# A three-part float32 product on one core: cross terms that read the upper halves of the float32r words in place

## The chip, the cores and the metric

The kernel runs on one core of one Trainium2 chip. The metric is the device time of one execution in microseconds. Three runs of the kernel before took 2292.56, 2293.05 and 2294.24 us: median 2293.05. One execution was recorded by the hardware profiler; its own time was 2294.02 us, and the span of its trace is 2292.2 us. The terms PE (TensorE's products), PEld (its weight loads), DVE (VectorE), ACT (ScalarE), POOL (GpSimd) and SP (SyncE, which issues the DMAs) are those of the profile.

## What is computed

For 8 sequences of 4096 tokens with 192 channels, a convolution with 7 taps per token and head (the taps are a softmax of `weight_gen`), and then a feed-forward layer with the activation h cos h:

```python
w = np.exp(weight_gen - max) ; w = w / (sum(w) + 1e-9)        # per token, head: 7 taps
attn = einsum('bshk,bskhg->bshg', w, the 7 last tokens of x)   # 8 heads of 24 channels
x = attn.reshape(32768, 192)
h = x @ w_in            # 192 x 2048
g = h * np.cos(h)
out = g @ w_out         # 2048 x 192
```

The weights `w_in` and `w_out` come as 64-bit floats; the kernel reads their words as integers and makes float32 values of them.

## The kernel before, in words

**Precision.** PE multiplies float32r words (float32 storage, rounded) or bf16 half-words. To come near float32, each factor is split in two: a high part in float32r and a low part, the rest, in bf16. A product x w is then x_hi w_hi in float32r plus two cross terms in bf16, x_lo times w_hi and x_hi times w_lo. A bf16 product needs both factors in bf16, so the high parts exist twice: `x_hi` (float32r) and `x_b` (a bf16 copy of it), `wa_hi` and `wa_b`, `wb_hi` and `wb_b`. The weight copies are made once, by `two_parts` (L118 to L144): ACT writes the high part (L141) and, if asked, the bf16 copy (L143), and POOL the low part (L144). The copy of x is made in `split` (L294 to L302) for each piece: ACT rounds to x_hi (L296), POOL writes x_b (L298 to L300), POOL or DVE writes x_lo (L301).

**Tiling.** The 32768 tokens are worked in NB = 64 batches of 512 tokens. The 2048 columns of `w_in` are 16 chunks of 128, taken as 8 pairs, so the main loop (L575) has 64 x 8 = 512 steps i, and some more to drain. PE works with two halves of 64 rows beside each other; the 192 channels are three pieces of 64 rows. `wa_*` holds channels so that a pair of products covers two of the three pieces, `wb_*` the remaining one of each chunk.

**One step on PE** (`products`, L597). `ffn_in_first` (L330) makes the first chunk's share: 3 pairs of products of 512 columns, in the order wa_b with x_lo, wa_lo with x_b, wa_hi with x_hi (L339). `ffn_in_second` (L345) makes 6 pairs (L356): wa_b x_lo, wa_lo x_b, wb_b x_lo, wb_lo x_b, wa_hi x_hi, wb_hi x_hi. `ffn_out` (L407, products at L430) multiplies what was finished LAG = 8 steps earlier: per step 8 pairs of 384 columns with the float32r part `ghi`, and 8 pairs of 192 columns with the bf16 part `glo`. In three of four steps the order is: the float32r part and half of the bf16 part of `ffn_out`, then `ffn_in_first`, the other half, `ffn_in_second`. In every fourth it is `ffn_in_first`, all of `ffn_out`, `ffn_in_second`. In a row of transposes (L318) PE also turns two rows of a later batch in spare columns of the accumulator.

**Beside PE.** For each step ACT writes the rounded number of turns (L366), the sine (L374) and the float32r part of g (L384); DVE the fraction of a turn (L370), the product g (L377) and the low part (L388). ACT also empties and clears accumulators (L446, L447, L452). POOL computes the attention of a later batch (L255 and L270), the split of the transposed rows (L298, L301) and the sum of the two halves of the output (L461).

**Order.** The program's order on every engine is the order in which the code emits it; manual dependencies at the end (L665 on) keep it. Each engine works its queue in that order. In the first steps the conversions of the later weight pieces are spread over steps 1 to 8 by the list `late` (L501), between the other work of ACT, DVE and POOL. Batches 1 and 2 are transposed whole and split at step 5 of the batch before (L591, L639), the later ones row by row.

Of the kernel before, what the change touches and what calls it, by code (L numbers as in the profile page):

```python
# [11 lines left out]
F32 = mybir.dt.float32  # L12
# [3 lines left out]
BF16 = mybir.dt.bfloat16  # L16
AF = mybir.ActivationFunctionType
ALU = mybir.AluOpType
AX = mybir.AxisListType

P = 128
# [22 lines left out]
def tile_softmax_conv_then_cos_ffn(  # L44
# [8 lines left out]
    nc = tc.nc  # L53
# [5 lines left out]
    F = w_in.shape[1]  # L59
# [4 lines left out]
    CT = R * P  # L64
# [13 lines left out]
    const = ctx.enter_context(tc.tile_pool(name="const", bufs=1))  # L78
    gpool = ctx.enter_context(tc.tile_pool(name="gpool", bufs=12))
    work = ctx.enter_context(tc.tile_pool(name="work", bufs=2))  # L80
# [12 lines left out]

    wa_hi = const.tile([P, F], F32R, name="wa_hi")
    wa_lo = const.tile([P, F], BF16, name="wa_lo")
    wa_b = const.tile([P, F], BF16, name="wa_b")

    wb_hi = const.tile([P, F // 2], F32R, name="wb_hi")  # L100
    wb_lo = const.tile([P, F // 2], BF16, name="wb_lo")
    wb_b = const.tile([P, F // 2], BF16, name="wb_b")
    wo = const.tile([P, NFC, 2 * D], F32R, name="wo")
    wo_b = const.tile([P, NFC, D], BF16, name="wo_b")

    def words(n):

        raw = gpool.tile([P, 2 * CW], I32, name="raw", tag="ghi")
        return raw[:, 0:2 * n]
# [8 lines left out]
    def two_parts(raw, hi, lo, half=None):  # L118
        shape = hi.shape[1:]
        n = math.prod(shape)  # L120

        def shaped(t, steps):
            t = t.rearrange("p (n s) -> p n s", s=steps)
            return t if len(shape) == 1 else t.rearrange("p (a b) s -> p a b s", b=shape[1])

        low, top = (shaped(raw, 2)[..., k] for k in range(2))
        size, bits = (shaped(t[:, 0:n], 1)[..., 0] for t in room.pop(0))
        nc.scalar.activation(out=size.bitcast(F32), in_=top.bitcast(F32), func=AF.Abs, scale=F64_SCALE)
        yield
        nc.vector.tensor_scalar(  # L130
            out=size, in0=size, scalar1=3, scalar2=None, op0=ALU.logical_shift_left)
        yield

        nc.vector.scalar_tensor_tensor(
            out=size, in0=top, scalar=-0x80000000, in1=size, op0=ALU.bitwise_and, op1=ALU.bitwise_or)
        yield

        nc.vector.scalar_tensor_tensor(
            out=bits, in0=low, scalar=29, in1=size, op0=ALU.logical_shift_right, op1=ALU.bitwise_or)
        yield  # L140
        nc.scalar.copy(out=hi, in_=bits.bitcast(F32))  # L141
        if half is not None:
            nc.scalar.copy(out=half, in_=bits.bitcast(F32))  # L143
        nc.gpsimd.tensor_tensor(out=lo, in0=bits.bitcast(F32), in1=hi.bitcast(F32), op=ALU.subtract)  # L144

    def w_in_a(c0, c1):
        raw = words(c1 - c0)
        for n in range(2):
            nc.sync.dma_start(out=raw[n * D2:(n + 1) * D2],
                              in_=w_in[n * P:n * P + D2, c0:c1].bitcast(I32))  # L150
        return two_parts(raw, wa_hi[:, c0:c1], wa_lo[:, c0:c1], wa_b[:, c0:c1])

    w_in_odd_even = w_in.rearrange("k (a n c) -> n k a c", n=2, c=P)

    def w_in_b(j):
        raw = words(CW)
        pairs = slice(j * CW // P, (j + 1) * CW // P)
        for n in range(2):
            nc.sync.dma_start(out=raw[n * D2:(n + 1) * D2].rearrange("k (a c) -> k a c", c=2 * P),
                              in_=w_in_odd_even[1 - n, D2:P, pairs, :].bitcast(I32))  # L160
        cols = slice(j * CW, (j + 1) * CW)
        return two_parts(raw, wb_hi[:, cols], wb_lo[:, cols], wb_b[:, cols])

    w_out_v = w_out.rearrange("(c p) d -> p c d", p=P)

# [120 lines left out]
    def parts_of(b):  # L286
        if b not in xT:
            hi = work.tile([P, 2, CT], F32R, name="x_hi")
            lo = work.tile([P, 2, CT], BF16, name="x_lo")
            near = work.tile([P, 2, CT], BF16, name="x_b")  # L290
            xT[b] = (hi, lo, near)
        return xT[b]

    def split(b, t, cs, eng):  # L294
        hi, lo, near = parts_of(b)
        nc.scalar.copy(out=hi[:, :, cs], in_=t)  # L296
        yield
        nc.gpsimd.tensor_scalar(  # L298
            out=near[:, :, cs], in0=hi[:, :, cs].bitcast(F32), scalar1=1.0, scalar2=1.0,
            op0=ALU.mult, op1=ALU.mult)  # L300
        eng.tensor_tensor(  # L301
            out=lo[:, :, cs], in0=t, in1=hi[:, :, cs].bitcast(F32), op=ALU.subtract)  # L302

# [136 lines left out]
    def evacuate(j):  # L440
# [13 lines left out]
        if k in (1, 3) and row:  # L454
            bt, r = row
            splits.append(split(bt, t, slice(r * P, (r + 1) * P), nc.gpsimd))
# [38 lines left out]
    def all_of(*steps):  # L495
# [4 lines left out]

    late = [  # L501
        (-1, 1, w_in_a, (768, 1280)), (-1, 2, w_in_b, (1,)), (-1, 2, w_out_2, (0,)),
        (0, 3, w_in_a, (1280, 1792)), (0, 3, w_out_2, (1,)), (1, 4, w_out_2, (2,)),
        (1, 4, w_out_2, (3,)), (2, 5, w_in_a, (1792, 2048)),
        (2, 5, w_out_2, (4,)), (4, 6, w_out_2, (5,)), (4, 7, w_out_2, (6,)),
        (5, 8, w_out_2, (7,)),
# [16 lines left out]
    next(sm0)  # L523
    load_rows(0)
    w_b0 = w_in_b(0)
    w_a0 = w_in_a(0, 256)
    sm1 = softmax(R, 3 * R, nc.gpsimd)
# [7 lines left out]
    def go_on(steps, n):  # L535
        for _ in range(n):
# [4 lines left out]
                      t=own_taps.rearrange("p (r h) k -> p r h k", h=H))  # L541
# [17 lines left out]
    go_on(w_a1, 1)  # L559
    all_of(mix_v)  # L560
    first = split(0, transpose_all(0), slice(0, CT), nc.vector)
    go_on(sm2, 2)
    go_on(w_a1, 3)
# [11 lines left out]
    for i in range(N + LAG + 1):  # L575
# [60 lines left out]
        if whole is not None:  # L636
            t = work.tile([P, 2, CT], F32, name="part", bufs=2)
            nc.scalar.copy(out=t, in_=whole)
            later.append(split(b + 1, t, slice(0, CT), nc.vector))  # L639
# [64 lines left out]
```

## Time and profile before

| | |
|---|---|
| median of the runs | 2293.05 us (2292.56 to 2294.24) |
| profiled execution, own time | 2294.02 us |
| its span | 2292.2 us |
| mean granted TensorE clock | 0.984 |
| busy: PE, PEld, DVE, ACT, POOL | 2187.0, 1679.2, 1903.1, 1860.6, 1860.8 us |
| DMA: HBM read, written | 76.50 MB, 25.17 MB |

How to read the lines. In a group, "out<-in" names the tiles, then partitions x elements and type, the count, busy time and mean nanoseconds of one, and the idle time just before with what ended it. "64*128" are the rows and columns of PE that a product uses. In a timeline a line has the start, the length, the engine, the line of the code, and in brackets how long the engine had been idle and what it had waited for. The starts and ends of products are modelled: they are pipelined, so the starts of two that follow each other say more than the length of one. A wait names an engine and line, then the one it waited for: total, times, longest.

### The profile page before, as it was taken

How to read it: one execution, taken by the hardware profiler on the slowest of the kernel's cores; microseconds unless marked ns; L12 is line 12 of the kernel's file. 1: busy time of each engine (PE TensorE's matmuls, PEld its weight loads, DVE VectorE, ACT ScalarE, POOL GpSimd, SP SyncE). 2: the span in 40 equal slices, each digit the busy share in tenths (PEclk: the TensorE clock that was granted, in tenths of full speed). 3: DMA queues.
4: the chain of work that ended last, by engine and by line, in shares of the span. 5: the costliest groups of instructions: out<-in, count | busy, mean ns of one | idle time of the engine just before them, and what ended most of it. 6: DMA issues, size and time to landing. Idle time of an engine off the chain costs nothing.

```text
span 2292.2 us, 61619 instructions
## 1 busy us (share of the span) xinstructions
PE 2187.0 (95%) x26472; PEld 1679.2 (73%) x26472; DVE 1903.1 (83%) x1644; ACT 1860.6 (81%) x2254; POOL 1860.8 (81%) x1583
## 2 busy tenths in 40 slices
PE   2699999999999999999999999999999999999998
PEld 1477777777777777777777777777777777777777
DVE  7788888878888888888888888888888888888886
ACT  4688888888888888887888888888888888888885
POOL 8788878888888878879888888878879888788730
PEclk8799999999999999999999999999999999999999
DMA  6221221211211221221211211111121211212100
GB/s 154 56 54 29 50 54 29 58 46 29 58 47 37 50 49 35 50 55 29 58 40 36 54 40 47 47 43 44 47 49 38 54 33 46 54 33 48 29 15 18
DMA packets 34847, 105.61 MB, mean 46 GB/s; under 512 B 3742, under 2 KB 23702, under 8 KB 34574
## 3 DMA queue, kind: packets, MB, share of 16 engines
q1 hardware_dynamic: 34574, 101.68, 18.5%
q8 instruction: 207, 3.39, 0.6%
q14 instruction: 66, 0.54, 0.1%
HBM read 76.50 MB, written 25.17 MB: 44 GB/s over the span
## 4 chain that ended last, share of the span: by engine, by line
PE 83%; ACT 7%; DVE 7%; issue 2%; POOL 1%; DMA 0%; SPq 0%; ACTq 0%; DVEq 0%
PE acc L430 42%; PE h L356 25%; PE h L339 13%; DVE turn L370 3%; ACT turn L366 3%; DVE glo L388 2%; ACT part L452 1%; PE acc L318 1%; ACT turn L374 1%; ACT ghi L384 1%; DVE den L214 1%; ACT acc L447 0%; ACT xrow L446 0%; POOL xa L270 0%; PE h L430 0%
## 5 line engine op out<-in xcount | busy, mean ns | idle before, releaser
L370 DVE TENSOR_TENSOR turn<-h,turn 128x1024 f32<-128x1024 f32 x512 | 625.9, 1222 | 302.0 <-ACT turn L366 301.9
L430 PE MATMUL acc<-wo,ghi 64*128 64x384 f32 x8096 | 821.6, 341 | 3.6 <-ACT acc L447 2.5
L430 PEld LDWEIGHTS acc<-wo,ghi 64*128 64x128 f32 x8096 | 726.2, 186 | 89.0 <-ACT acc L447 56.4
L270 POOL TENSOR_TENSOR xa<-xa,pr 128x768 f32<-128x768 f32 (+1 forms) x384 | 698.2, 1818 | 0.7
L374 ACT ACTIVATE turn<-turn 128x1024 f32<-128x1024 f32 x512 | 542.0, 1059 | 186.6 <-DVE turn L370 184.8
L366 ACT ACTIVATE turn<-h 128x1024 int32<-128x1024 f32 x512 | 525.9, 1027 | 194.3 <-PE h L356 176.9
L377 DVE SCALAR_TENSOR_TENSOR h<-h,turn 128x1024 f32<-128x1024 f32 x512 | 631.0, 1232 | 54.4 <-ACT turn L374 54.4
L388 DVE TENSOR_TENSOR glo<-h,ghi 128x1024 bf16<-128x1024 f32 x512 | 622.0, 1215 | 10.1 <-ACT ghi L384 10.1
L255 POOL TENSOR_TENSOR pr<-xt,taps 128x768 f32<-128x768 f32 (+1 forms) x384 | 588.3, 1532 | 8.3
L384 ACT CAST ghi<-h 128x1024 fp32r<-128x1024 f32 x512 | 516.7, 1009 | 9.7 <-DVE h L377 9.7
L430 PE MATMUL acc<-wo_b,glo 64*128 64x192 bf16 x8096 | 489.0, 245 | 0.1
L430 PEld LDWEIGHTS <-glo 64*128 64x128 bf16 (+1 forms) x8128 | 315.9, 95 | 118.6 <-issue 100.5
L298 POOL TENSOR_SCALAR x_b<-x_hi 128x256 bf16<-128x256 f32 (+1 forms) x247 | 102.9, 417 | 261.8 <-ACT x_hi L296 261.8
L339 PE MATMUL h<-x_hi,wa_hi 64*128 64x512 f32 x1024 | 302.9, 587 | 0.0
L356 PE MATMUL h<-x_hi,wa_hi 64*128 64x512 f32 x1024 | 302.7, 586 | 0.0
L339 PE MATMUL h<-x_lo,wa_b 64*128 64x512 bf16 x1024 | 198.3, 382 | 71.0 <-DVE glo L388 66.1
L356 PE MATMUL h<-x_hi,wb_hi 64*128 64x512 f32 x1024 | 205.5, 396 | 0.0
L461 POOL TENSOR_TENSOR fin<-part 128x384 f32<-128x384 f32 x126 | 128.1, 1016 | 86.2 <-ACT part L452 86.2
L356 PE MATMUL h<-x_lo,wa_b 64*128 64x512 bf16 x1024 | 196.8, 379 | 0.8
L339 PE MATMUL h<-x_b,wa_lo 64*128 64x512 bf16 x1024 | 197.2, 380 | 0.0
L356 PE MATMUL h<-x_b,wa_lo 64*128 64x512 bf16 x1024 | 197.0, 380 | 0.0
L356 PE MATMUL h<-x_lo,wb_b 64*128 64x512 bf16 x1024 | 196.8, 379 | 0.0
(78 smaller groups left out, 1869.2 us busy)
## 6 DMA issues: line engine op xcount, KB each, us to landing
xt<-in_x_dram SPq DMA_DIRECT2D x62, 960.0 KB, 6.9
out_dram<-fin SPq DMA_DIRECT2D x128, 192.0 KB, 2.5
taps<-in_weight_gen_dram SPq DMA_DIRECT2D x15, 448.0 KB, 4.7
raw<-in_moe_w_out_dram SPq DMA_DIRECT2D x8, 384.0 KB, 4.4
raw<-in_moe_w_in_dram SPq DMA_DIRECT2D x10, 256.0 KB, 9.7
xt<-in_x_dram SPq DMA_DIRECT2D x1, 768.0 KB, 9.9
xt<-in_x_dram SPq DMA_DIRECT2D x1, 540.0 KB, 5.4
raw<-in_moe_w_in_dram SPq DMA_DIRECT2D x4, 128.0 KB, 5.0
```

The lines of the kernel that those rows point to most:

```text
L255: eng.tensor_tensor(out=dst.rearrange("p r (h g) -> p r h g", h=H), in0=xt[:, k + ra:k + rb, :].rearrange("p r (h g) -> p r h g", h=H), in ...
L270: eng.tensor_tensor(out=acc if k < K else xa, in0=acc, in1=old[:, ra:rb], op=ALU.add)
L339: nc.tensor.matmul(h[:, q, :], lhsT=w[rs, chunk(pair, q)], rhs=v[rs, q, :], start=(m == 0), stop=False, skip_group_check=True)
L356: nc.tensor.matmul(h[:, 1 - q, :], lhsT=w[rs, cs], rhs=v[rs, q ^ middle, :], start=False, stop=(m == len(prods) - 1), skip_group_check=True)
L366: nc.scalar.activation(out=t.bitcast(I32), in_=hs[i], func=AF.Identity, bias=0.25, scale=1.0)
L370: nc.vector.tensor_tensor(out=t, in0=hs[i], in1=t.bitcast(I32), op=ALU.subtract)
L374: nc.scalar.activation(out=t, in_=t, func=AF.Sin, bias=SIN_BIAS, scale=SIN_SCALE)
L377: nc.vector.scalar_tensor_tensor(out=hs[i], in0=hs[i], scalar=TWO_PI, in1=turns.pop(i), op0=ALU.mult, op1=ALU.mult)
L384: nc.scalar.copy(out=hi, in_=hs[i])
L388: nc.vector.tensor_tensor(out=lo, in0=hs.pop(i), in1=hi.bitcast(F32), op=ALU.subtract)
L430: nc.tensor.matmul(to, lhsT=g[rs, n, t * P:(t + 1) * P], rhs=w[rs, fc, :], start=(lo == 0 and c == 0 and (k == 0 or whole and k == 1)), st ...
L461: (nc.vector if last else nc.gpsimd).tensor_tensor(out=fin, in0=part[:, :, 0:D], in1=part[:, :, D:2 * D], op=ALU.add)
```

## The change

The three bf16 copies are no longer made. In their place stands a view: the float32r words are read as bf16 half-words with a step of two, starting at the upper half of the first word. A float32's upper 16 bits are a bf16 number, the value cut off instead of rounded. So `wa_b` and `wb_b` are views of `wa_hi` and `wb_hi`, and `near` (before: tile `x_b`) is a view of `x_hi`; the products keep their order and shapes, and their operands in bf16 now lie four bytes apart. In `split` POOL's instruction for `x_b` is gone, and `two_parts` is called for `w_in` without a third target, so that its ACT copy is gone too; for `w_out` it stays (`wo_b`).

```diff
+    def tops(t):
+
+        return t.bitcast(BF16).rearrange("p (n two) -> p n two", two=2)[:, :, 1]
+
     wa_hi = const.tile([P, F], F32R, name="wa_hi")
     wa_lo = const.tile([P, F], BF16, name="wa_lo")
-    wa_b = const.tile([P, F], BF16, name="wa_b")
+    wa_b = tops(wa_hi)
...
-    wb_b = const.tile([P, F // 2], BF16, name="wb_b")
+    wb_b = tops(wb_hi)
...
-        return two_parts(raw, wa_hi[:, c0:c1], wa_lo[:, c0:c1], wa_b[:, c0:c1])
+        return two_parts(raw, wa_hi[:, c0:c1], wa_lo[:, c0:c1])
...
-        return two_parts(raw, wb_hi[:, cols], wb_lo[:, cols], wb_b[:, cols])
+        return two_parts(raw, wb_hi[:, cols], wb_lo[:, cols])
...
-            near = work.tile([P, 2, CT], BF16, name="x_b")
+            near = tops(hi.rearrange("p q c -> p (q c)")).rearrange("p (q c) -> p q c", q=2)
...
         nc.scalar.copy(out=hi[:, :, cs], in_=t)
         yield
-        nc.gpsimd.tensor_scalar(
-            out=near[:, :, cs], in0=hi[:, :, cs].bitcast(F32), scalar1=1.0, scalar2=1.0,
-            op0=ALU.mult, op1=ALU.mult)
         eng.tensor_tensor(
             out=lo[:, :, cs], in0=t, in1=hi[:, :, cs].bitcast(F32), op=ALU.subtract)
```

## The prediction

> **What bounds the kernel now.** I read the page first: busy times, then the chain that ended last, then the busy time by stretch, and only then single instructions.
>
> ```profile
> PE 2187.0 (95%) x26472; PEld 1679.2 (73%) x26472; DVE 1903.1 (83%) x1644; ACT 1860.6 (81%) x2254; POOL 1860.8 (81%) x1583
> ...
> PE 83%; ACT 7%; DVE 7%; issue 2%; POOL 1%; DMA 0%; SPq 0%; ACTq 0%; DVEq 0%
> ```
>
> TensorE (PE) carries 83% of the chain, GpSimd (POOL) 1%. The busy time by stretch shows where the remaining 17% lie:
>
> ```profile
> 40.00:60.00 20.00, 9.58 (x42) 4.12 (x42) 15.68 (x20) 12.99 (x21) 19.66 (x15) 0.59 0.11 34
> 60.00:100.00 40.00, 23.55 (x138) 13.35 (x138) 29.88 (x38) 21.30 (x33) 28.40 (x20) 0.62 0.21 55
> ...
> 400.00:1000.00 600.00, 589.07 (x7240) 454.53 (x7236) 504.58 (x427) 499.73 (x605) 507.82 (x430) 0.99 0.19 47
> ```
>
> The columns are the stretch, its length, then busy time (and count) of PE, PEld, DVE, ACT, POOL, then the granted clock. There are two regimes. Up to 100 us PE is half idle (9.58 of 20) at a granted clock of 0.6; there the work of the other engines sets the pace. From then on PE is busy for 589 of 600 us: what is saved on another engine there is worth nothing, and what is added on PE costs all of itself. So I take the change in those two parts: the removed copies matter only in the start, the new reads only in the long run. Who waits for whom between 130 and 2230 us confirms it:
>
> ```profile
> POOL x_b L298 <- ACT x_hi L296: 251.6, 96, 7.1
> ...
> PEld acc L430 <- ACT acc L447: 56.4, 122, 0.6
> ...
> PE h L339 <- DVE glo L388: 37.8, 16, 2.5
> ```
>
> PE waits for ScalarE's clearing of the accumulator and, 16 times, for VectorE's low part. It never waits there for GpSimd. GpSimd itself stands 251.6 us in front of x_b, waiting for ScalarE's x_hi.
>
> **The change part by part. The removed copies.**
>
> ```profile
> L298 POOL TENSOR_SCALAR x_b<-x_hi 128x256 bf16<-128x256 f32 x244 | 99.8, 409 | 258.7 <-ACT x_hi L296 258.7
> ...
> L298 POOL TENSOR_SCALAR x_b<-x_hi 128x1024 bf16<-128x1024 f32 x3 | 3.1, 1047 | 3.1 <-ACT x_hi L296 3.1
> ...
> L143 ACT CAST wa_b<-t 128x512 bf16<-128x512 f32 x3 | 1.9, 619 | 0.0
> ...
> L143 ACT CAST wb_b<-t 128x512 bf16<-128x512 f32 x2 | 1.2, 622 | 0.0
> ...
> L143 ACT CAST wa_b<-t 128x256 bf16<-128x256 f32 x2 | 0.8, 408 | 0.0
> ```
>
> The 244 narrow x_b, 99.8 us, all lie in the long run. They go off POOL and nothing ends sooner: the wait of 251.6 us moves to x_lo, the next POOL instruction of the same split, and PE has no row that waits for either. The cover is PE itself, busy 98% of that stretch. Worth: 0. The copies of the start are 3.1 us on POOL and 1.9 + 1.2 + 0.8 = 3.9 us on ACT, 7.0 us if every one were on the path. These are the places where the timeline shows that they are:
>
> ```profile
> 26.24 0.62 ACT L141 CAST wa_hi<-t 128x512 fp32r<-128x512 f32 x1
> ...
> 26.38 1.05 POOL L298 TENSOR_SCALAR x_b<-x_hi 128x1024 bf16<-128x1024 f32 x1 [0.31 <-ACT x_hi L296]
> ...
> 27.39 1.27 POOL L144 TENSOR_TENSOR wa_lo<-t,wa_hi 128x512 bf16<-128x512 f32 x1
> ...
> 45.49 1.27 POOL L144 TENSOR_TENSOR wa_lo<-t,wa_hi 128x512 bf16<-128x512 f32 x1
> ...
> 46.79 1.02 ACT L366 ACTIVATE turn<-h 128x1024 int32<-128x1024 f32 x1 [4.79 <-POOL wa_lo L144]
> ...
> 49.12 0.63 ACT L143 CAST wb_b<-t 128x512 bf16<-128x512 f32 x1
> 49.64 0.52 ACT L141 CAST wo<-t 128x384 fp32r<-128x384 f32 x1
> ...
> 51.56 1.23 DVE L377 SCALAR_TENSOR_TENSOR h<-h,turn 128x1024 f32<-128x1024 f32 x1 [1.36 <-ACT turn L374]
> ...
> 57.06 0.63 ACT L143 CAST wa_b<-t 128x512 bf16<-128x512 f32 x1
> ...
> 57.58 0.52 ACT L141 CAST wo<-t 128x384 fp32r<-128x384 f32 x1
> ...
> 59.51 1.23 DVE L377 SCALAR_TENSOR_TENSOR h<-h,turn 128x1024 f32<-128x1024 f32 x1 [0.73 <-ACT turn L374]
> ```
>
> First, POOL. Without x_b the wa_lo of 27.39 can start when its wa_hi is done, 26.24 + 0.62 = 26.86: 0.53 us sooner. POOL then works through the attention of batch 1 without a pause up to the wa_lo of 45.49, for which ACT's turn waited 4.79 us. So 0.53 us reaches ACT at 46.79. Second, ACT. The cast wb_b held up what follows it by 49.64 - 49.12 = 0.52 us, and DVE waited 1.36 us for the ACT turn behind it; the cast wa_b held up by 57.58 - 57.06 = 0.52, and DVE waited 0.73. Two more times 0.52. The four casts before 40 us are at no cost, since VectorE is the later one there:
>
> ```profile
> 23.30 1.94 PE L309 MATMUL h<-ident,xa 128*128 128x128 f32 x8 [23.30 <-DVE xa L270]
> ...
> 27.60 0.61 PE L339 MATMUL h<-x_lo,wa_b 64*128 64x512 bf16 x2 [2.36 <-DVE x_lo L301]
> ```
>
> ```profile
> 38.61 1.22 DVE L370 TENSOR_TENSOR turn<-h,turn 128x1024 f32<-128x1024 f32 x1
> ...
> 39.25 0.61 ACT L143 CAST wa_b<-t 128x512 bf16<-128x512 f32 x1
> ...
> 39.86 1.06 ACT L374 ACTIVATE turn<-turn 128x1024 f32<-128x1024 f32 x1
> ```
>
> PE's first work waits for VectorE's attention, its first product for VectorE's x_lo, and the cast of 39.25 ends with VectorE's turn (38.61 + 1.22 = 39.83), which ACT needs next. The seventh, a narrow one, I leave out. Sum 0.53 + 0.52 + 0.52 = 1.57 us. The ends are 0 (if PE's products, slow at a clock of 0.6, end last at each of these places) and 7.0 us. I take 1.57 since each of its three terms has a wait row behind it. What is gained by 100 us is kept to the end, as PE then runs without a pause.
>
> **The change part by part. The new reads.** No instruction is added, and no wait. The products that read x_b now move every second half-word of x_hi: wa_lo with x in the first and second half, wb_lo with x, 3 pairs (two row halves run beside each other) in each of 512 steps, 1536 pairs. The products with x_lo now load their weights (wa_b twice, wb_b once) from every second half-word: again 3 in each step. The trace of before has no read of two bytes with a step of four. The nearest row for the stream is float32r, four bytes with a step of four.
>
> ```profile
> 1007.26 0.38 PE L356 MATMUL h<-x_lo,wa_b 64*128 64x512 bf16 x2
> ...
> 1007.91 0.38 PE L356 MATMUL h<-x_b,wb_lo 64*128 64x512 bf16 x2
> ```
>
> and in the chain in order of time:
>
> ```profile
> 1020.11 1.33 PE h L356 x12
> 1021.43 1.41 PE acc L430 x16
> ```
>
> From 1007.26 to 1007.91 three bf16 pairs start, 0.217 us each, or 0.42 ns a column. The six pairs of L356 take 1.33 us, so its two float32r pairs take (1.33 - 4 x 0.217) / 2 = 0.231. The eight float32r pairs of 384 columns take 1.41 us, 0.176 each. Those 128 columns are 0.055 us, 0.43 ns a column: the stream of four-byte words is not slower by the column; what float32r costs more, 0.014 us a pair, it costs as a fixed amount. The bounds for one stepped pair are therefore 0 and 0.014 us, for all 1536 of them 0 and 22 us. I take 0, because the rate by the column, which is what a step would touch, is that of bf16 within 3%. A gain is excluded: the pair already starts at the pace of its columns.
>
> For the weight load the nearest rows are the packed bf16 load and the float32r load of the same 128 columns:
>
> ```profile
> L356 PEld LDWEIGHTS h<-x_hi,wa_hi 64*128 64x128 f32 x1024 | 99.3, 189 | 60.9 <-issue 1.8
> ...
> L356 PEld LDWEIGHTS <-wa_b 64*128 64x128 bf16 x1024 | 51.9, 95 | 5.5 <-issue 5.5
> ```
>
> A stepped load lies between 95 and 189 ns by these. Behind a product of 512 columns (217 ns) either is hidden. It can show only where the product ahead is short: the wa_b loads right behind the 192-column products with glo, that is in L356 of the 504 steps that follow the first 8 and so have an output product, and in L339 of three of four of them, 378: some 880 loads. What a slow load costs there can be read at the end of the kernel, where a float32r load follows such products:
>
> ```profile
> 2278.13 0.10 PEld L430 LDWEIGHTS <-glo 128*128 128x128 bf16 x1
> 2278.21 0.19 PEld L430 LDWEIGHTS h<-wo,ghi 128*128 128x128 f32 x1
> ...
> 2278.32 0.37 PEld L430 LDWEIGHTS h<-wo,ghi 128*128 128x128 f32 x2
> ```
>
> Packed loads follow each other in 0.08 us, the pace of 192 columns; the float32r load frees the way for the next after 0.11. So 0.03 us is exposed, and 880 x 0.03 = 26 us; by the bare difference of durations, 0.094, it would be 83. I take 0, the packed row: the stepped load has its type and its count of elements, and differs from the float32r load in the type. The bounds are 0 and 26, with 83 as the far end.
>
> **Sum.** The profiled execution took 2294.02 us (span 2292.2). 2294.02 - 1.57 + 0 + 0 = 2292.45. The median shown is 2293.05, so 0.97 lower, and the forecast for the median is 2293.05 - 1.57 = 2291.5, a change of 0.07%. A measurement of this kernel can tell about 0.2%, or 4.6 us, from no change; the forecast is no change.
>
> **The rivals.** *The stepped weight load is slow* (slower). Place: the 880 wa_b loads behind 192-column products. It decides as soon as such a load takes over 80 ns of the load path, and at the float32r rows' 0.11 us it costs 26 us: 2293.05 - 1.57 + 26 = 2317; the 122 steps in which PE waits for ACT's clearing anyhow (56.4 us, 0.46 each) would hide two loads each, 7 us at most, which I leave in the price. For it speaks that bytes, and not the type, may make 189 out of 95: then a load that spans 512 bytes pays as float32r does. Against it, that type and bytes change together between those two rows, so the type alone explains them as well. [...] Chance 0.19.
>
> *The stepped stream is slow* (slower). With the float32r pair's fixed cost on 1536 pairs, 22 us: 2313, chance 0.10. If the stream fell to half the rate, 1536 x 0.217 = 333 us: about 2625. The float32r rows speak against that: they fetch the same span of bytes at full pace. Chance 0.04.
>
> *The start gives more* (faster). If all 7.0 us of copies lie on the path up to 100 us, 2286. For it: ACT and POOL are each a releaser there in turn. Against: four of the seven casts run while VectorE is later. Chance 0.09.
>
> *The copies are not what they seem*: that the views still cause a copy would show as a row on L298 or L143 for w_in; the diff leaves none, chance 0.01, 2293.
>
> **How the numbers follow.** The forecast has 0.57; its own range is 2289 to 2293. Slower by over 0.2% is 0.19 + 0.10 + 0.04 = 0.33. Faster by over 0.2% is the rival with 0.09. Within 0.2% is 0.57 + 0.01 = 0.58. The range goes from 2287, just short of the whole 7.0 us, to 2317, the load rival at its tail price; beyond lie the halved stream, half of the load rival and half of the faster one, about 0.18.
>
> **What would show each step.** Right: L298 gone and x_lo waiting some 250 us for x_hi; loads of wa_b and wb_b at 95 ns; L356's six pairs still 1.33 us in the chain; the wait of PE for VectorE and ACT unchanged; PE's first full stretch a microsecond or two sooner. Wrong: loads from wa_hi by half-words near 189 ns and the first pair of L356 starting later behind glo (the load rival), or pairs of wa_lo starting over 0.217 us apart (the stream rival). A gain of over 5 us with PE's pairs unchanged would mean that I misread who is late in the start.

## The result, and the profile after

The changed kernel took 2306.26 us (median of 4 runs, 2304.72 to 2306.81), the kernel before 2293.64 us beside it (2292.56 to 2294.43). The ratio is 1.0054, with a 95% interval of 1.0037 to 1.0072: 12.6 us slower. The forecast was no change, 2291.5 us. The profiled execution took 2306.81 us, its span 2305.0 us.

First the busy times and the chain on the page of the changed kernel:

```profile
PE 2201.8 (96%) x26472; PEld 1691.3 (73%) x26472; DVE 1903.3 (83%) x1644; ACT 1857.8 (81%) x2247; POOL 1769.5 (77%) x1336
...
PE 79%; issue 6%; POOL 5%; DVE 5%; ACT 4%; DMA 0%; SPq 0%; ACTq 0%; POOLq 0%; DVEq 0%
```

GpSimd lost 1860.8 - 1769.5 = 91 us and ScalarE 3 us, as the copies are gone. PE has the same 26472 products and is 14.8 us busier. So the time came to PE, with no work added. The waits between 130 and 2230 us of the changed kernel:

```profile
POOL x_lo L302 <- ACT x_hi L300: 275.6, 121, 7.6
...
PEld acc L431 <- ACT acc L448: 51.3, 121, 0.6
...
PE h L340 <- POOL xa L274: 34.6, 14, 2.5
...
PE h L340 <- DVE glo L389: 2.1, 1, 2.1
```

GpSimd's wait moved from x_b to x_lo, as foreseen. PE's wait of 14 times 2.5 us has a new name, POOL xa, but the old size (37.8 us before, 34.6 + 2.1 now). A wait is put down to what ended last, and here two things end nearly together; an experiment below tells whether the new name means anything.

On the chain GpSimd now has 5% where it had 1%; the same experiment bears on that. The group of one product, before, and the groups of the same product and of a stepped load, after; then the spread of that product's duration (smallest, median, largest, in ns), before and after:

```profile
L356 PE MATMUL h<-x_b,wa_lo 64*128 64x512 bf16 x1024 | 197.0, 380 | 0.0
```

```profile
L357 PE MATMUL h<-x_hi,wa_lo 64*128 64x512 bf16 x1024 | 203.4, 390 | 0.0
...
L357 PEld LDWEIGHTS <-wa_hi 64*128 64x128 bf16 x1024 | 53.2, 95 | 5.6 <-issue 5.6
```

```profile
L356 PE MATMUL h<-x_b,wa_lo x1024: 373/376/631, 29.5 to 2267.6; 64*128 64x512 bf16 x171
```

```profile
L357 PE MATMUL h<-x_hi,wa_lo x1024: 383/386/631, 30.5 to 2280.7; 64*128 64x512 bf16 x171
```

The stepped weight load still takes 95 ns. The product whose moving side is stepped takes 10 ns more. The starts of successive pairs in the changed kernel say the same:

```profile
1010.15 0.38 PE L357 MATMUL h<-x_lo,wa_hi 64*128 64x512 bf16 x2
1010.37 0.39 PE L357 MATMUL h<-x_hi,wa_lo 64*128 64x512 bf16 x2
1010.60 0.38 PE L357 MATMUL h<-x_lo,wb_hi 64*128 64x512 bf16 x2
1010.81 0.39 PE L357 MATMUL h<-x_hi,wb_lo 64*128 64x512 bf16 x2
```

A packed pair is followed after 0.22 and 0.21 us, the stepped one after 0.23. A second thing changed on PE. Behind the idle stretch of each softmax step PE runs some time at half its clock, in some of the steps. The stretches of 6 us behind such idle stretches in a row, first three before, then five after; the third number from the right is the granted clock:

```profile
474.80:480.80 6.00, 5.65 (x52) 5.12 (x54) 4.82 (x5) 2.88 (x3) 5.60 (x8) 0.72 0.31 69
613.00:619.00 6.00, 4.86 (x62) 4.43 (x64) 5.61 (x5) 4.16 (x5) 5.60 (x8) 1.00 0.48 106
751.20:757.20 6.00, 5.60 (x52) 5.00 (x54) 4.87 (x5) 2.94 (x3) 5.60 (x8) 0.72 0.32 70
```

```profile
477.40:483.40 6.00, 4.62 (x58) 4.04 (x60) 5.85 (x5) 4.13 (x5) 5.60 (x8) 1.00 0.55 124
616.30:622.30 6.00, 5.63 (x52) 5.03 (x54) 4.85 (x5) 2.91 (x3) 5.60 (x9) 0.72 0.35 77
755.70:761.70 6.00, 5.58 (x52) 4.99 (x54) 4.89 (x5) 2.95 (x3) 5.60 (x9) 0.72 0.34 74
895.30:901.30 6.00, 5.65 (x52) 4.95 (x54) 4.82 (x5) 2.88 (x3) 5.60 (x9) 0.72 0.32 72
1034.00:1040.00 6.00, 4.79 (x60) 4.25 (x62) 5.68 (x5) 4.13 (x5) 5.60 (x8) 1.00 0.49 105
```

A mean of 0.72 over 6 us is half clock for 6 x 0.28 / 0.5 = 3.4 us, which costs 1.7 us of PE's time: in the stretch from 340.51 to 343.92 us of the changed kernel the pairs at 343.25 and 343.68 us start 0.43 us apart, against 0.22 at full clock. Each of the two traces has 15 such idle stretches after 130 us. By the trace's record of the granted clock, half clock follows 7 of them before (from the third on, every second one) and 11 after (three of four for the most part). So there were two candidates, 10 ns on each stepped product and four more stretches of half clock, 4 x 1.7 = 6.8 us.

### The profile page after: what moved, and what is told of

Read it like the earlier page. It is cut to its first block, busy times and chain, and to the rows that moved or that the text cites. A ratio compares the mean times of both kernels' runs of the same rounds, so it can differ in the third digit from the quotient of the medians.

```text
span 2305.0 us, 61365 instructions
## 1 busy us (share of the span) xinstructions
PE 2201.8 (96%) x26472; PEld 1691.3 (73%) x26472; DVE 1903.3 (83%) x1644; ACT 1857.8 (81%) x2247; POOL 1769.5 (77%) x1336
## 4 chain that ended last, share of the span: by engine, by line
PE 79%; issue 6%; POOL 5%; DVE 5%; ACT 4%; DMA 0%; SPq 0%; ACTq 0%; POOLq 0%; DVEq 0%
PE acc L431 41%; PE h L357 25%; PE h L340 13%; DVE turn L371 2%; POOL pr L259 2%; ACT turn L367 2%; POOL xa L274 1%; PE acc L319 1%; POOL xa L259 1%; POOL x_lo L302 1%; ACT part L453 1%; ACT turn L375 1%; DVE glo L389 1%; DVE den L218 1%; PE h L431 0%
## 5 line engine op out<-in xcount | busy, mean ns | idle before, releaser
L340 PE MATMUL h<-x_hi,wa_hi 64*128 64x512 f32 x1024 | 310.2, 599 | 0.0
L357 PE MATMUL h<-x_hi,wa_hi 64*128 64x512 f32 x1024 | 306.8, 592 | 0.0
L302 POOL TENSOR_TENSOR x_lo<-xrow,x_hi 128x256 bf16<-128x256 f32 x122 | 90.0, 738 | 249.5 <-ACT x_hi L300 246.1
L340 PE MATMUL h<-x_lo,wa_hi 64*128 64x512 bf16 x1024 | 199.7, 383 | 70.6 <-POOL xa L274 34.6
L340 PE MATMUL h<-x_hi,wa_lo 64*128 64x512 bf16 x1024 | 203.8, 391 | 0.0
L357 PE MATMUL h<-x_hi,wa_lo 64*128 64x512 bf16 x1024 | 203.4, 390 | 0.0
L357 PE MATMUL h<-x_hi,wb_lo 64*128 64x512 bf16 x1024 | 202.2, 387 | 0.0
L357 PE MATMUL h<-x_lo,wa_hi 64*128 64x512 bf16 x1024 | 198.6, 380 | 0.8
```

Source lines behind the costliest of these rows:

```text
L340: nc.tensor.matmul(h[:, q, :], lhsT=w[rs, chunk(pair, q)], rhs=v[rs, q, :], start=(m == 0), stop=False, skip_group_check=True)
L357: nc.tensor.matmul(h[:, 1 - q, :], lhsT=w[rs, cs], rhs=v[rs, q ^ middle, :], start=False, stop=(m == len(prods) - 1), skip_group_check=True)
```

## Experiments

Theory A is that each stepped moving product costs PE some 10 ns more. Theory B is that the stepped weight loads cost it. Theory C is that the missing GpSimd copy shifts the other engines against PE. Two later questions are what about the step costs, and how much of the 12.6 us is the clock.

### Only the moving side stepped

```diff
-            near = work.tile([P, 2, CT], BF16, name="x_b")
+            near = tops(hi.rearrange("p q c -> p (q c)")).rearrange("p (q c) -> p q c", q=2)
...
-        nc.gpsimd.tensor_scalar(
-            out=near[:, :, cs], in0=hi[:, :, cs].bitcast(F32), scalar1=1.0, scalar2=1.0,
-            op0=ALU.mult, op1=ALU.mult)
```

> Only x_b becomes a stepped view of x_hi; the bf16 weight copies stay packed and are made by ACT as before. Theory A (each stepped moving product costs PE some 10 ns more, the stepped weight loads nothing): 1536 pairs at about 9 ns, 12 to 16 us slower than before, 2305 to 2309. Theory B (the stepped weight loads cost it): 0 to 1 us faster than before. Theory C (the removed GpSimd copy shifts the other engines' work so that PE waits more): slower by as much as in the whole change, but with pairs of wa_lo and x_hi still 0.216 us apart.

2304.44 us against 2293.43, ratio 1.0046 (1.0032 to 1.0059): 11.0 us slower, half a microsecond under the range of theory A, and far from theory B.

```profile
L357 PE MATMUL h<-x_hi,wa_lo x1024: 384/385/631, 29.8 to 2278.1; 64*128 64x512 bf16 x171
```

The stepped product has its 10 ns here too, with packed weights around it. The moving side alone brings the loss.

### Only the weights stepped

```diff
-    wa_b = const.tile([P, F], BF16, name="wa_b")
+    wa_b = tops(wa_hi)
...
-    wb_b = const.tile([P, F // 2], BF16, name="wb_b")
+    wb_b = tops(wb_hi)
```

> Only wa_b and wb_b become stepped views (ACT's copies for w_in gone); x_b is copied by GpSimd and read packed. Theory A: same as before, 0 to 2 us faster (2291 to 2294). Theory B: 12 to 15 us slower, 2306. Theory C: same as before.

2290.14 us against 2293.43, ratio 0.9985 (0.9976 to 0.9994): 3.3 us faster, a little more than expected.

```profile
L360 PEld LDWEIGHTS <-wa_hi x1024: 92/94/148, 29.2 to 2264.1; 64*128 64x128 bf16 x171
...
L360 PE MATMUL h<-x_b,wa_lo x1024: 373/376/631, 29.9 to 2264.4; 64*128 64x512 bf16 x171
```

Theory B falls: the loads take what packed ones took. This is also the version that beats both kernels, by 0.15%: take the weights as views, and keep the copy of x.

The two runs do not add up to the whole change: 11.0 - 3.3 = 7.7 us, not 12.6. The clock is a part of that. These two traces have 10 and 6 stretches of half clock, 3 more and 1 less than before, where the changed kernel has 4 more; the two missing ones are 3.4 of the 4.9 us.

### The GpSimd copy gone, nothing moving stepped

The weight views, and an x_b in one packed tile that is written for batch 0 alone:

```diff
-            near = work.tile([P, 2, CT], BF16, name="x_b")
+            near = once
...
+        if b == 0:
             nc.gpsimd.tensor_scalar(
```

> Weight views as in the change; x_b is a packed tile that is written once, from batch 0, and never again, so GpSimd's 246 other copies are gone and the cross term of w_lo uses batch 0's x in all batches (that part of the result is left out). Nothing is read stepped by the moving side. Theory A: 0 to 3 us faster than before, 2290 to 2293.5. Theory C: slower by about 12 us as the whole change, since the same GpSimd work is gone.

2291.4 us against 2293.43, ratio 0.9989 (0.9981 to 0.9998). Its waits between 130 and 2230 us:

```profile
PE h L346 <- POOL xa L274: 35.1, 14, 2.5
PE h L346 <- DVE glo L395: 3.5, 2, 2.1
```

The new name is there as in the changed kernel, and GpSimd has its 5% of the chain here too, but the 12 us are not lost. Theory C falls as their source; the name shows only what ended last. Removing the 246 other copies gains nothing over the run before it, as PE never waited for them: this kernel is 1.3 us slower than that one. One wait of PE at 130 us is longer by 0.8 us without the copy; it comes up again below.

### The order of the six pairs

```diff
-        prods = ((wa_b, x_lo, 0), (wa_lo, x_b, 0), (wb_b, x_lo, 1), (wb_lo, x_b, 1),
+        prods = ((wa_b, x_lo, 0), (wb_b, x_lo, 1), (wa_lo, x_b, 0), (wb_lo, x_b, 1),
```

> The whole change, with the six pairs of ffn_in_second in another order: wa_b x_lo, wb_b x_lo, wa_lo x_b, wb_lo x_b, then the float32r ones, so that no stepped product is followed by a packed one there. If each stepped product costs by itself (by column or fixed): same as the changed kernel, 2306. If the price is paid at the switch from a stepped stream to a packed one: 3 to 6 us less, 2300 to 2303.

2306.24 us against 2293.43, ratio 1.0054 (1.0041 to 1.0066), the same as the changed kernel. The price belongs to the stepped product, not to a switch from stepped to packed.

### A step of two, four and eight in a tile of its own

```diff
+    once = const.tile([P, 2 * CT * 4], BF16, name="x_b")
+    once = once.rearrange("p (q c s) -> p q c s", q=2, s=4)[:, :, :, 0]
```

(here for four), written once from batch 0.

> As the kernel with the packed x_b that is written once (batch 0's values in all batches, so the cross term of w_lo is left out for the others), but its half-words lie two apart in a tile of their own; the other half-words are never written, and x_hi's words are read by the float32r products alone. If the step itself costs: the same 12 to 14 us over the packed form as in the change, 2303 to 2306, pairs 0.227 us. If the cost comes from reading the same words as the float32r products: as the packed form, 2290 to 2292.

2310.05 us against 2292.91, ratio 1.007 (1.0053 to 1.0086): 4 us over the range, and over the changed kernel. Some 2.4 of them lie where the stepped pair of wb_lo stands ahead of a float32r pair: by the mean distances of starts the two take 460 ns here, 456 in the changed kernel and 450 before, once in each of 512 steps. The rest stays open.

> The same with a step of four half-words (8 bytes; x_b from batch 0 alone, as before). If the price is a fixed one for any step: 2303 to 2306, as step two. If it grows with the span read (packed 1 kB, step two 2 kB, step four 4 kB: one, then three times the extra): pairs of about 0.25 us, 1536 x 0.033 = 51 us, about 2340. [...]

2593.01 us, ratio 1.1302 (1.1285 to 1.1318).

> A step of eight half-words, 16 bytes; one tile of 512 columns serves both row halves (x_b from batch 0 and its first half alone). If fixed: 2303 to 2306. If it grows with the span: seven times the extra, pairs of 0.29 us, about 2400. [...]

3264.95 us, ratio 1.4232 (1.421 to 1.4253). The product's duration at steps two, four and eight (one fence for each kernel):

```profile
L363 PE MATMUL h<-x_b,wa_lo x1024: 383/385/632, 29.8 to 2283.6; 64*128 64x512 bf16 x171
```

```profile
L363 PE MATMUL h<-x_b,wa_lo x1024: 607/608/634, 30.4 to 2566.3; 64*128 64x512 bf16 x171
```

```profile
L364 PE MATMUL h<-x_b,wa_lo x1024: 1054/1055/1082, 31.5 to 3237.8; 64*128 64x512 bf16 x171
```

and the start of that pair and of the next, at step four and at step eight:

```profile
1003.47 0.62 PE L363 MATMUL h<-x_b,wa_lo 64*128 64x512 bf16 x2
1003.90 0.41 PE L363 MATMUL h<-x_lo,wb_hi 64*128 64x512 bf16 x2
```

```profile
1004.15 1.07 PE L364 MATMUL h<-x_b,wa_lo 64*128 64x512 bf16 x2
1005.03 0.41 PE L364 MATMUL h<-x_lo,wb_hi 64*128 64x512 bf16 x2
```

The step itself costs, with no float32r product near its words: step two in its own tile has the 385 ns of the view. From four on the time doubles with the step: 0.43 and 0.88 us for 512 columns. In bytes spanned in a partition that is 4096 / 0.43 = 9.5 kB/us and 8192 / 0.88 = 9.3 kB/us, one rate. Packed bf16 asks for 1024 / 0.216 = 4.7 kB/us, half of it, so by this estimate the fetch does not hold it up. Step two spans 2048 bytes; at the packed pace of 0.216 us that would be 9.5 kB/us, the whole of that rate with nothing to spare, and it gets 2048 / 0.227 = 9.0 (0.227 us is the median distance of the starts). My expectations for the growth with the span (0.25 and 0.29 us) were far too low; they took the 11 ns as a slope.

### Halves of 256 columns

```diff
+    def pieces(halved):
+        n = 2 if halved else 1
+        return [(slice(k * CT // n, (k + 1) * CT // n), q) for k in range(n) for q in range(2)]
...
-            for q in range(2):
+            for c, q in pieces(v is x_b):
```

> Weight views as in the change, x_b copied and packed, but each of the 1536 product pairs that read x_b is made as two of 256 columns: 1536 pairs more, each of half the length. It serves as the packed base for the next; the doubled loads (95 ns each) stay hidden behind 107 ns. Two or three ns more a pair: 2294 to 2298.

2299.18 us against 2293.33, ratio 1.0028 (1.0016 to 1.0041), a microsecond over the range.

> The changed kernel with its 1536 stepped product pairs made as two of 256 columns each. If the step's price is by the column: 12 to 14 us over the packed halves. If it is fixed for each product: twice that, 24 to 28 us over the packed halves.

2308.68 us beside it, ratio to the kernel before 1.007 (1.0055 to 1.0085): 9.5 us over the packed halves, less than the 12 to 14 expected and far from 24. The whole times are no clean measure here, as the stepped run has 11 stretches of half clock and the packed one 8; the starts are. Two half products and the pair after them, packed and then stepped:

```profile
1001.26 0.38 PE L364 MATMUL h<-x_b,wa_lo 64*128 64x256 bf16 x4
1001.48 0.38 PE L364 MATMUL h<-x_lo,wb_hi 64*128 64x512 bf16 x2
```

```profile
1001.31 0.39 PE L361 MATMUL h<-x_hi,wa_lo 64*128 64x256 bf16 x4
1001.54 0.38 PE L361 MATMUL h<-x_lo,wb_hi 64*128 64x512 bf16 x2
```

512 columns in two pieces cost 0.22 us packed and 0.23 stepped. On average over the long run it is 218 and 230 ns, 12 more, as in one piece (216 and 228). The price goes by the column; a fixed price would have doubled. At the two other places, ahead of a float32r pair, it did not grow either (4 and 1 ns, against 10 and 5 in one piece).

### Without the stretches of half clock

The exponential of the 14 in-loop softmaxes becomes a copy, in the kernel before and in the changed one:

```diff
-        nc.scalar.activation(out=t, in_=t, func=AF.Exp)
+        nc.scalar.activation(out=t, in_=t, func=AF.Exp if early else AF.Copy)
```

> The kernel before, with ACT's Exp in the 14 softmaxes of the main loop that are not the early ones replaced by a copy of the same size (the exponential of those taps is left out). ACT then loads no function table in the loop (two of 1.28 us each time), so PE's idle stretch of about 2.5 us in each softmax should go and with it the stretches of half clock behind it. Base for the next: some 45 to 55 us under the kernel before, about 2243, steps of over 6.4 us gone.

> The changed kernel with the same replacement. If the extra time of the change is the steady price of the stepped streams (about 15 ns a step, 7 to 8 us) plus about three more stretches of half clock (2.3 us each): 6 to 9 us over the kernel before with the same replacement. If it is the stepped streams alone: 12 to 18 us over it, as with the softmax.

2283.13 and 2294.77 us; ratios to the kernel before 0.9957 (0.9944 to 0.9971) and 1.0002 (0.9993 to 1.0011). This missed its aim. Only 10 us went, and PE still idled, as the waits of the first show:

```profile
PE h L339 <- DVE glo L388: 31.3, 15, 2.1
ACT part L452 <- PE acc L430: 27.4, 15, 1.8
```

The idle stretch has another source than ScalarE's table loads (the kernel before has 15 at L203 and 15 at L374, 1.28 us each, this one none there): in the step behind the exponential the code emits the step's products ahead of ScalarE's ghi (`early_sums`, L622), and ScalarE then waits for the accumulator. With it stayed steps at half clock, 4 and 7 of them, and the difference of 11.6 us. So the two causes were still not apart, and the order was put right as well:

```diff
-        early_sums = busy and step == EXP + 1
+        early_sums = False
```

> The kernel before with the exponential of the 14 in-loop softmaxes replaced by a copy (left out, as in the runs with the same edit) and with the order of the step behind it as in all other steps, so that ACT does not wait for the accumulator before it writes ghi. PE's idle stretch of 2.1 us there should go, and with it every stretch of half clock: 14 x about 2.3 us and the 4 stretches of 2.4 less than the run with the copy alone, 2240 to 2255. Base for the next.

> The changed kernel with the same two edits. No stretch of half clock in either: what remains of the difference to the base is the steady price of the stepped streams. By the step lengths of the two first profiles (33.64 and 33.79 us for 8 steps) 512 x 0.015 to 0.02 = 8 to 10 us, less the 1 to 2 us of the start: 6 to 9 us. If the clock stretches have no part in it: 12 us as before.

2243.38 us (2242.99 to 2243.98) and 2249.76 us (2248.69 to 2251.12); ratios to the kernel before 0.9779 (0.9765 to 0.9793) and 0.9807 (0.9793 to 0.9821). After the first 100 us neither runs at half clock (1.00 granted in each stretch read from 100 to 2000 us), and PE's waits for glo are 0.7 and 1.3 us in all (130 to 2230 us). The difference is now 6.4 us, inside the range of 6 to 9. ScalarE's first instruction of steps 64 and 480, without and with the change:

```profile
336.74 1.03 ACT L366 ACTIVATE turn<-h 128x1024 int32<-128x1024 f32 x1 [0.77 <-PE h L356]
...
2088.87 1.03 ACT L366 ACTIVATE turn<-h 128x1024 int32<-128x1024 f32 x1 [0.77 <-PE h L356]
```

```profile
337.67 1.03 ACT L367 ACTIVATE turn<-h 128x1024 int32<-128x1024 f32 x1 [0.80 <-PE h L357]
...
2095.56 1.03 ACT L367 ACTIVATE turn<-h 128x1024 int32<-128x1024 f32 x1 [0.81 <-PE h L357]
```

Over 416 steps that is 4.2119 and 4.2257 us a step: 13.8 ns, or 7.1 us in 512 steps; 6.4 were measured. The start's gain is not seen in this pair: at step 64 the changed kernel is 0.93 us behind, and 64 steps at 13.8 ns make 0.88. So about half of the 12.6 us is the steady price of the stepped streams, and the other 6 went with the idle stretches. The counts of half clock give the same: 6.4 + 4 x 1.7 = 13.2 for the 12.6 us of the change, and 6.4 + 3 x 1.7 = 11.5 for the 11.6 us of the pair before this one.

What decides which idle stretches are followed by half clock can be read from the same traces. Every stretch of half clock behind them lasts 3.41 us, and within a trace their starts lie whole multiples of 3.413 us apart: 475.98, 752.46 and 1028.94 us before (81 multiples each), 340.51, 616.99, 756.93 and 896.88 after (81, 41 and 41). Two pieces of this grid around two idle stretches of the changed kernel, each with the piece behind it:

```profile
337.10:340.51 3.41, 1.33 (x14) 1.21 (x16) 2.82 (x4) 2.85 (x4) 3.41 (x4) 1.00 1.00 248
340.51:343.92 3.41, 3.41 (x34) 3.03 (x32) 3.14 (x3) 1.76 (x2) 3.01 (x6) 0.50 0.05 9
477.04:480.45 3.41, 1.68 (x18) 1.55 (x20) 3.04 (x3) 2.85 (x4) 3.41 (x3) 1.00 1.03 245
480.45:483.86 3.41, 3.41 (x50) 2.95 (x48) 2.80 (x3) 2.11 (x3) 3.01 (x6) 1.00 0.02 2
```

Both idle stretches last 2.5 us. Of the first, 2.08 us fall into one piece of the grid, and the next piece runs at half clock; of the second 1.73 us, and nothing follows. Eleven traces have these 15 idle stretches (all but those of step four, step eight and the last pair). Where 2.02 us or more fell into one piece, half clock followed every time, 92 times; where it was 1.97 us or less, never, 73 times. So it is the place on the grid that decides, and the change moves that: an idle stretch with no half clock behind it is followed by the next after 137.4 us before and 137.9 after, as 32 steps that are each 13.8 ns longer lie between them.

## Why the prediction was wrong

**The bounds of the kernel** were right: PE carries the long run, and what it was given there, it cost.

**The removed copies** were right in place, and in size as far as 59 us. The long run lost 91 us of GpSimd's work and gained nothing. In the start of the changed kernel:

```profile
24.28 1.94 PE L310 MATMUL h<-ident,xa 128*128 128x128 f32 x8 [24.28 <-DVE xa L274]
...
47.30 1.02 ACT L367 ACTIVATE turn<-h 128x1024 int32<-128x1024 f32 x1 [4.32 <-POOL wa_lo L148]
...
51.56 1.23 DVE L378 SCALAR_TENSOR_TENSOR h<-h,turn 128x1024 f32<-128x1024 f32 x1 [0.84 <-ACT turn L375]
...
58.94 1.23 DVE L378 SCALAR_TENSOR_TENSOR h<-h,turn 128x1024 f32<-128x1024 f32 x1 [0.16 <-ACT turn L375]
```

This execution's first PE work came 24.28 - 23.30 = 0.98 us later. At the ACT turn it was 0.51 late, at the first DVE row level, at the second 0.57 early: gains of 0.47, 0.51 and 0.57 against the forecast terms of 0.53, 0.52 and 0.52. What the prediction did not see is that a missing copy can also cost. In the split of batch 2, which is made whole, GpSimd goes on with the attention at once; VectorE's x_lo beside it takes 2.68 us (L302) in place of 1.97 (L301), its glo ends later, and PE stands longer. PE's next product, before and after:

```profile
130.07 0.39 PE L339 MATMUL h<-x_lo,wa_b 64*128 64x512 bf16 x2 [0.65 <-DVE glo L388]
```

```profile
129.17 0.39 PE L340 MATMUL h<-x_lo,wa_hi 64*128 64x512 bf16 x2 [1.30 <-DVE glo L389]
```

That takes back 0.65 of the 1.55 us. With the weights alone stepped, where the copy of x stays, the two casts were worth 1.0 us by the forecast's terms, and the kernel was 3.3 us faster. One stretch of half clock less, 6 against 7, can be 1.7 of that; the rest is not resolved.

**The weight loads** were right: 0, with loads of 95 ns. The load rival, at 0.19, falls.

**The stepped stream** is the step that failed: "I take 0, because the rate by the column, which is what a step would touch, is that of bf16 within 3%". I had read the float32r pair's extra 0.014 us as a fixed amount and set a difference of 3% by the column to nothing. But 3% of a pair that is made 1536 times is not nothing here: 0.217 x 0.03 x 1536 = 10 us. The runs show a price by the column, 0.216 to 0.227 us, 5%, which would be 17 us on all 1536 pairs. By the mean distances of starts in the last two traces it is 12 ns at this pair, 10 at the pair of the first half and 5 at that of wb_lo, the last two together with the float32r pair behind them: 27 ns a step, or 14 us in 512. The bounds of 0 and 22 us held it. What arrives is 7.1 us. PE's loads wait 5.1 us less for ScalarE's clearing (51.3 against 56.4 us), which would hide that much; the last 2 I cannot place. The stream rival, at 0.10 and 2313 us, had the right place, the wrong kind of price (fixed instead of by the column) and a size too large by half (22 us against 14).

**Not in the sum at all** was the clock. The last 6 us are stretches of half clock behind idle stretches of PE that both kernels have; the change alters hardly anything in them but when they fall. That they go when the idle stretches go is shown by the last pair of runs, and that their place on the grid of 3.41 us decides, by the eleven traces. How many there are follows from the distance between the idle stretches, and not from stepped reads as such: the weights alone have 6, the packed halves 8, the changed kernel 11.

The measured time lies inside the range of 2287 to 2317, but the likeliest case and the sign were wrong.

## What to carry to other kernels

A view that saves a copy can move its cost to whoever reads it: here 91 us of GpSimd's work went without a gain, and the stepped streams cost 7.1 us on PE. The products' time grew with the bytes that their moving operand spans in a partition: 0.216 us packed (1024 bytes), then 0.227, 0.43 and 0.88 us for 2048, 4096 and 8192, while the stepped weight loads took the 94 ns of packed ones. So compare the span that a product must fetch in its time with the span of the packed form, and take the weights, not the moving side, as stepped views. When an engine is busy 98% of the time, a difference of a few per cent in a repeated row is a term of the sum and not a rounding. And where a kernel has regular idle stretches on PE, look at the granted clock behind them, and count the stretches of half clock before and after: here a step 13.8 ns longer came with 11 of them in place of 7.

## What the runs showed of the hardware

The moving operand came at about 9.4 kB/us in each partition, gaps included, at steps of four and of eight half-words (4096 bytes in 0.43 us, 8192 in 0.88); packed bf16 took 0.216 us for 512 columns, half of that rate, and every second half-word took 0.227, 9.0 kB/us, 5% more time. A stepped weight load of 128 columns took 94 ns, a packed one of the same kernel 94. Behind idle stretches of 2.1 to 2.5 us half clock came in pieces of 3.41 us on one grid in each trace, and some 2.0 us of idle PE inside one piece brought it in the next (2.02 us did, 1.97 did not).
